# Row maxima from bfloat16 halves, paired float32 score products, and weights joined by exclusive or, in a fused attention and feed-forward kernel

## The chip, the cores and the metric

The kernel runs on one core of a Trainium2 chip. The metric is the time of one execution in device microseconds. Before the change the median of three runs is 602.51 us (601.61 to 602.69). All times here are those of runs and of one profiled execution of the kernel on the chip.

## The reference

Attention over 4 batches, 8 heads, 768 positions and head dimension 64, then a feed-forward layer on its output. Every position sees the first `n_global` = 8 positions and the `n_local` = 96 positions up to itself; each head has a linear bias of its own slope.

```
scores = scale * q @ k.T + bias          # bias = -slope[h] * distance
scores = where(is_global | is_local, scores, -1e9)
a = exp(scores - max); a = a / (sum(a) + 1e-9)
x = (a @ v), heads side by side          # 3072 tokens x 512
h = x @ w_in                             # 512 x 2048, float64
g = h / (1 + exp(-1.702 h))
out = (g @ w_out).astype(float32)        # 2048 x 512, float64
```

The inputs q, k, v are float32. The two weight matrices are float64, so that each of their numbers is two 32-bit words in memory.

## The kernel before, in words

**Planner.** Nearly all the work is a list of tasks. Each task names the engines that may do it with the microseconds that it is thought to take on each, the tasks that it follows, the buffers that it uses, and possibly a due time (`want`) or an earliest time (`soon`). `Work.order` (L104) passes due times back through the list, adds a shift for each group of tasks by its tag (`NUDGE`, L30), and then plays the work through once: at each moment every free engine takes the ready task with the earliest due time whose buffers are free. `LAT` (L47) is the time that it reckons between the end of a task and the start of a task on another engine, and a transfer is reckoned to begin 1.2 us after its issue and to be visible 1.0 us after its end (L171-174). The resulting order is the order of the instructions on each engine. Nothing is reordered when the kernel runs: TensorE takes its matmuls in that order, and all transfers go out from SP's queue in that order, apart from a few. In the first 50 us (`WARM`) the planner gives TensorE filler matmuls (`spare`, L1057; tile `idle`, L1060) whenever it would have nothing to do.

**Attention, first blocks.** The 3072 rows are cut into 24 blocks of 128. Blocks 0 to 3 (`first`, L581) are the first block of each batch, which sees only itself. Their q and k are loaded as float32, turned by TensorE (L422) and scaled into `QZ` and `KF` (L429). Two heads share the 128 partitions, 64 each; `QZ` holds q of one head with zeros in the other's partitions, so that a product with `KF` gives one head. A block then takes these steps. For each head one float32 product (L604) and one bfloat16 product that adds the bias (L605) give the scores; VectorE takes the negated maximum of each row (L609); TensorE turns the maxima (L612). Then the same scores are made once more, transposed, by a float32 product with the operands changed over (L623), the bias (L624) and a product that subtracts the row's maximum (L625). ScalarE's exponential (L636) gives weights that are already turned, and TensorE multiplies them by the values (L631). The result is normalised (`finish`, L653), turned (L689) and split into two float16 halves (L692, L693).

**Attention, other blocks.** Blocks 4 to 23 run in units of two heads (`unit`, L519): scores by float16 halves (L536), row maximum with bias (L542), exponential (L552), split in halves (L556, L557), transfer that turns the tile (L558), values (L567 to L569).

**Weights.** The 16 pieces of 1 MB (`weights`, L357; `w_in` and `w_out` for each of 8 steps) come in through three buffers `ws`. Each float64 is made a float32 from its words: VectorE shifts the high word by 3 (L370, into `wa`); the sign with a fixed exponent goes into the upper half of another tile, on VectorE or ScalarE, whichever the planner picks (L373, L374); ScalarE puts the top bits of the low word in the lower half of it (L375); VectorE adds the two as integers (L376); ScalarE and VectorE then split the sum into float16 halves (L377, L378). The other products of the feed-forward layer use these halves in three products each.

**Feed-forward layer.** The first three chunks of 256 rows are multiplied directly (`up`, L787; `down`, L895). The other nine use a scheme with seven products in place of eight (`up_two`, L827), for which `twist` (L727) forms sums of the weight pieces. The last group of sums overwrites the high-word pieces of four steps (L767, L769).

**Checks.** Squares of q, k, v and of the weights (L404, L998, L1006) and other sums are gathered into one flag, and a general version at the end runs only when the flag says that the inputs are out of the range for which this version holds.

Of the kernel before, what the change touches and what calls it, by code (L numbers as in the profile page):

```python
# [19 lines left out]
P = 128  # L20
# [9 lines left out]
NUDGE = {"T2": -1.5, "down02": 1.4, "down05": -8.2, "down07": -0.8, "down103": 6.7, "down113": -5.5,  # L30
# [9 lines left out]
FIRST = 4  # L40
SIGN = [{"DVE": 0.62, "ACT": 1.0}]
# [5 lines left out]
LAT = 0.3  # L47
MM128, MM256, MM512, MM64, FP128, FP65, TURN = 0.056, 0.109, 0.216, 0.029, 0.216, 0.113, 0.11
# [39 lines left out]
class Work:  # L88
# [15 lines left out]
    def order(self):  # L104
# [25 lines left out]
        while len(done) < len(self.tasks) + spared:  # L130
            moved = False
            for e in free:
# [77 lines left out]
def kernel(  # L210
# [133 lines left out]
    m0 = add({"DVE": 1.3}, distances, [m0], [ints, flt, mk], -4.0)  # L344
    late = add({"POOL": 1.0}, lambda e: None, [m0], want=0.0)
    m0 = add({"DVE": 0.65}, counts, [m0, late])
    covers = add({"DVE": 1.2}, covered, [m0])
    covers.soon = 300.0
    m1 = add({"DVE": 1.1}, own, [m0], [flt, mk])
    M1 = [add({"DVE": 0.6, "ACT": 1.0}, lambda e, f=f: slopes(e, slice(2, 3), range(4 * f, 4 * f + 4)), [m1], [mk]) for f in range(2)]  # L350
    m2 = add({"DVE": 0.7}, other, [m1], [flt, mk])
    M2 = add({"DVE": 2.3, "ACT": 2.6}, lambda e: slopes(e, slice(0, 2)), [m2], [mk])


    WT, W_ready = {}, {}

    def weights(s, u):  # L357
# [7 lines left out]
        part = lambda z: w().bitcast(U16).rearrange("p z (c t) -> p (z c) t", t=2)[:, :, z]  # L365
        t0 = add({"SP": 3.2}, lambda e: load_weights(nc, ws(), w_in, w_out, s, u), bufs=[ws])
# [3 lines left out]
        t2 = add({"DVE": 0.62}, lambda e: nc.vector.tensor_scalar(ai(), ws()[:, :, 1], 3, None, ALU.logical_shift_left),  # L370
                 [t0], [ws, wa])
        t3 = add(SIGN[(2 * s + u) % len(SIGN)], lambda e: (
            nc.vector.tensor_scalar(extra(), ws()[:, :, 1], -2 ** 31, 127 << 23, ALU.bitwise_and, ALU.bitwise_or) if e == "DVE"  # L373
            else nc.scalar.activation(part(1).bitcast(BF16), ws()[:, :, 1].bitcast(F32), AF.Sign)), [t0], [ws, w])  # L374
        t4 = add({"ACT": 1.21}, lambda e: nc.scalar.mul(part(0), ws()[:, :, 0].bitcast(U32), 2.0 ** -29), [t3], [ws, w])  # L375
        t5 = add({"DVE": 1.15}, lambda e: nc.vector.tensor_add(ai(), ai(), extra()), [t2, t3, t4], [w, wa])  # L376
        t6 = add({"ACT": 0.96}, lambda e: nc.scalar.mul(w()[:, 0], wa(), 2.0 * SW), [t5], [wa, w])  # L377
        t7 = add({"DVE": 1.15}, lambda e: nc.vector.scalar_tensor_tensor(  # L378
            w()[:, 1], wa(), 2.0 * SW, w()[:, 0], ALU.mult, ALU.subtract), [t6], [wa, w])
        W_ready[s, u] = t7  # L380

# [7 lines left out]
    blk, prev, checks = {}, {}, []  # L389
# [5 lines left out]
    def load(n, raw, parts=(0, 1, 2)):  # L395
        b, i = place(n)
        return [add({"SP": 1.55}, lambda e, z=z: nc.sync.dma_start(
# [10 lines left out]
    def prep_first(n):  # L408

        raw = Buf(r_raw, [P, 3, H, D], F32, f"raw{n}")  # L410
        QZ = Buf(r_w[NST - 1 - n // 2, n % 2], [P, NU, 2, P], F32, f"QZ{n}")
        KF = Buf(r_hl, [P, NU, P], F32, f"KF{n}", lambda t: t.bitcast(F32).rearrange("p (u t) -> p u t", u=NU))
        d = blk[n] = dict(QZ=QZ, KF=KF, sm=Buf(r_sm, [P, 2 * H], F32, f"sm{n}"))
        zero = add({"POOL": 1.0}, lambda e: [nc.gpsimd.memset(QZ()[D * z:D * z + D, :, 1 - z, :], 0.0) for z in range(2)], bufs=[QZ])
# [166 lines left out]
    def first(n, want):  # L581
# [7 lines left out]
        def products(h):  # L589

            if n < FIRST:
                return [(d["QZ"]()[:, h // 2, h % 2, :], d["KF"]()[:, h // 2, :])]
# [678 lines left out]
```

## Time and profile before

| what | value |
|---|---|
| median of three runs | 602.51 us (601.61 to 602.69) |
| span of the profiled execution, first to last instruction | 600.7 us |
| what lies around the span (runs less span) | 0.9 to 2.0 us |
| granted TensorE clock, mean | 0.997 |
| busy: TensorE, VectorE, ScalarE | 587.5, 503.0, 471.4 us |
| moved by the DMA queues | 109.58 MB, mean 182 GB/s |

The profiled execution's own time is not given beside its span; the runs show how much lies around a span. TensorE is busy for 98% of the span, but its matmuls overlap, and filler counts as busy too. A share of busy time is an average over the whole span; the stages, the timeline and the chain of waits tell more.

### The profile page before, as it was taken

What the parts mean: (1) busy time and instruction counts of PE and PEld (TensorE: products, weight loads), DVE (VectorE), ACT (ScalarE), POOL (GpSimd) and SP (SyncE); (2) the same over time, 40 slices, a digit from 0 to 9 for tenths busy, and PEclk for the clock granted to TensorE, in tenths of its full rate; (3) what the DMA queues carried; (4) which work ended last, traced back from release to release, by engine and by line L of the source; (5) the groups of instructions that cost most, each with busy time, mean ns of one, the idle gap of its engine ahead of it and who ended that gap; (6) DMA issues with size and microseconds to landing.
All of it is one profiled execution on the core that took longest, in us unless ns stands there. A gap on an engine that the chain in (4) does not pass through costs nothing.

```text
span 600.7 us, 17037 instructions
## 1 busy us (share of the span) xinstructions
PE 587.5 (98%) x6816; PEld 445.9 (74%) x6816; DVE 503.0 (84%) x1177; ACT 471.4 (78%) x1098; POOL 5.8 (1%) x18
## 2 busy tenths in 40 slices
PE   8989999999999999999999999999999999999996
PEld 5878767777777867777677777777678768867895
DVE  6998999999999999789699789798979978766532
ACT  3878899978768988888698899788999978944432
POOL 3000000000000000000000000000000000000000
PEclk9999999999999999999999999999999999999998
DMA  8998799999976768979996999999989999920001
GB/s 225 310 251 260 227 253 198 191 179 197 212 141 128 156 117 186 196 145 196 216 206 163 226 209 238 197 233 198 236 186 223 224 193 228 234 40 3 36 1 41
DMA packets 268502, 109.58 MB, mean 182 GB/s; under 512 B 249536, under 2 KB 250048, under 8 KB 268416
## 3 DMA queue, kind: packets, MB, share of 16 engines
q1 hardware_dynamic: 267984, 108.30, 86.6%
q8 instruction: 55, 0.90, 0.7%
q14 instruction: 31, 0.25, 0.1%
q10 hardware_dynamic: 432, 0.13, 0.1%
HBM read 57.67 MB, written 6.29 MB: 106 GB/s over the span
## 4 chain that ended last, share of the span: by engine, by line
PE 85%; DMA 7%; ACT 4%; DVE 2%; issue 1%; SPq 1%; POOL 0%; DVEq 0%; ACTq 0%; POOLq 0%
PE y L895 36%; PE pa L827 14%; PE h L787 10%; PE pb L827 10%; PE s L536 5%; DMA pt<-hl 3%; DMA QK<-QK 2%; PE s L604 1%; PE pv L567 1%; PE pv L569 1%; PE pv L568 1%; PE sT L623 1%; PE idle L1060 1%; DMA xT<-x 1%; DMA out_dram<-yo 1%
## 5 line engine op out<-in xcount | busy, mean ns | idle before, releaser
L895 PE MATMUL y<-w,g 128*128 128x512 f16 (+1 forms) x1248 | 266.8, 363 | 0.0
L895 PEld LDWEIGHTS <-g 128*128 128x128 f16 x1248 | 117.9, 98 | 103.3
L827 PEld LDWEIGHTS <-w 128*128 128x128 f16 x1728 | 101.3, 98 | 5.0
L552 ACT ACTIVATE p<-p,NM 128x232 f32<-128x232 f32 x160 | 76.4, 480 | 7.0 <-DVE NM L542 7.0
L827 PEld LDWEIGHTS <-T 128*128 128x128 f16 x1296 | 77.1, 98 | 6.0
L787 PE MATMUL h<-xT,w 128*128 128x256 f16 x576 | 69.4, 273 | 0.3 <-DMA xT<-x 0.2
L542 DVE CUSTOM_DVE_ANT_0 p<-s,mm 128x232 f32<-128x232 f32 x160 | 57.7, 395 | 8.2 <-PE s L536 7.3
L787 PEld LDWEIGHTS <-w 128*128 128x128 f16 x576 | 55.2, 98 | 9.3 <-issue 0.6
L557 DVE TENSOR_TENSOR hl<-p,hl 128x464 f16<-128x464 f32 x80 | 50.9, 636 | 10.2 <-ACT hl L556 10.1
L868 DVE SCALAR_TENSOR_TENSOR g<-t,g 128x512 f16<-128x512 f32 x72 | 49.3, 687 | 11.1 <-ACT g L867 10.9
L867 ACT ACTIVATE g<-t 128x512 f16<-128x512 f32 x72 | 45.0, 628 | 9.5 <-DVE t L860 8.1
L556 ACT CAST hl<-p 128x464 f16<-128x464 f32 x80 | 46.1, 576 | 6.4 <-DMA pt<-hl 4.4
L859 ACT ACTIVATE t<-h 128x512 f32<-128x512 f32 (+1 forms) x72 | 35.9, 515 | 18.2 <-DVE h L835 15.1
L835 DVE TENSOR_TENSOR h<-pb,h 128x256 f32<-128x256 f32 x72 | 29.6, 420 | 23.0 <-PE pb L827 19.6
L827 PE MATMUL pa<-xS,T 128*128 128x128 f16 x648 | 45.0, 219 | 0.0
L860 DVE SCALAR_TENSOR_TENSOR t<-t,h 128x512 f32<-128x512 f32 (+1 forms) x72 | 38.2, 553 | 4.6 <-ACT t L859 4.0
L536 PEld LDWEIGHTS <-QK 128*128 128x128 f16 x640 | 36.5, 98 | 3.7 <-DMA QK<-QK 0.2
L536 PE MATMUL s<-QK 128*128 128x128 f16 x320 | 38.4, 219 | 0.1
L827 PE MATMUL pb<-xS,w 128*128 128x128 f16 x540 | 37.5, 219 | 0.0
L567 PE MATMUL pv<-VR,pt 128*128 128x64 f16 x288 | 34.8, 193 | 2.6 <-DMA pt<-hl 2.6
L827 PE MATMUL pa<-xT,w 128*128 128x128 f16 x540 | 37.0, 219 | 0.0
L569 PE MATMUL pv<-VR,pt 128*128 128x64 f16 x288 | 34.8, 193 | 0.0
(181 smaller groups left out, 1079.9 us busy)
## 6 DMA issues: line engine op xcount, KB each, us to landing
ws<-in_moe_w_in_dram SPq DMA_DIRECT2D x8, 1024.0 KB
ws<-in_moe_w_out_dram SPq DMA_DIRECT2D x8, 1024.0 KB
raw<-in_q_dram SPq DMA_DIRECT2D x24, 256.0 KB
raw<-in_k_dram SPq DMA_DIRECT2D x24, 256.0 KB
out_dram<-yo SPq DMA_DIRECT2D x22, 256.0 KB
QK<-QK SPq DMA_DIRECT2D x40, 128.0 KB
raw<-in_v_dram SPq DMA_DIRECT2D x20, 256.0 KB
ws_00again<-in_moe_w_in_dram SPq DMA_DIRECT2D x8, 512.0 KB
```

The source lines that it names most:

```text
L536: nc.tensor.matmul(sp()[:, j, lo:hi], d["QK"]()[:, 0, h, :], K[:, 1 + z, h, P - (hi - lo):], start=(z == 0), stop=(z == 1), skip_group_che ...
L542: nc.vector.tensor_tensor_reduce(out=pr()[:, j, :], in0=sp()[:, j, :], in1=m, scale=-1.0 / SC, scalar=3.0e38, op0=ALU.add, op1=ALU.min, ac ...
L552: ex.append(add({"ACT": 0.473}, lambda e, j=j: nc.scalar.activation(pr()[:, j, :], pr()[:, j, :], AF.Exp, bias=NM[:, n, hs[j]:hs[j] + 1], ...
L556: t4 = add({"ACT": 0.5}, lambda e: nc.scalar.copy(hl()[:, 0, :, SKIP:], pr()), ex, [pr, hl])
L557: t5 = add({"DVE": 0.55}, lambda e: nc.vector.tensor_sub(hl()[:, 1, :, SKIP:], pr(), hl()[:, 0, :, SKIP:]), [t4], [pr, hl])
L567: nc.tensor.matmul(o, ph, V[:, 0, h], start=(s == 0), stop=False, skip_group_check=True)
L569: nc.tensor.matmul(o, pl, V[:, 0, h], start=False, stop=(s == ns - 1), skip_group_check=True)
L787: nc.tensor.matmul(ph()[:, fi, :], w1(s, cc, z, fi), X[:, y, cc, :], start=(j + cc == 0), stop=(j == 2 and cc == NCC - 1))
L827: nc.tensor.matmul(o()[:, fi], w, x()[:, y * NCC + 2 * k + cc, t], start=(first and fi + j + cc == 0), stop=(last and j + cc == 3), skip_g ...
L867: t4 = add({"ACT": 0.53}, lambda e, g=g, tt=tt: nc.scalar.mul(g()[:, 0], tt(), SG / (SX * SW)), u, [tt, g])
L868: t5 = add({"DVE": 0.61}, lambda e, g=g, tt=tt: nc.vector.scalar_tensor_tensor(g()[:, 1], tt(), SG / (SX * SW), g()[:, 0], ALU.mult, ALU.s ...
L895: nc.tensor.matmul(y(), part(zg, f), w2(s, z, f % 2)[:, m], start=(begin and f + j == 0), stop=(end and j == 2 and f == 2 * len(steps) - 1 ...
```

## The change

1. **Row maxima from bfloat16.** In blocks 0 to 3 the scores from which the maxima are taken use the upper 16 bits of each float32 word of q and k, read in place as bfloat16 with a step of two. The transposed scores stay float32.
2. **Two heads in one product.** `QZ` is laid out with the two heads of a pair outermost, and the transposed scores of both heads come from one float32 product of 256 columns with `KF` as the stationary operand.
3. **Weights joined by exclusive or.** The sign step is always VectorE's; the separate shift is gone; one instruction shifts the high word and joins it to the rest by exclusive or. The low bits are scaled by 0.9365, so that they can't round up into the next bit. The exponent is then right without a factor of two.
4. **Checks.** The squares of the weights are taken with the weights themselves, four of them early, and the last sums of `twist` wait for them. Bounds of the checks are tighter.
5. **Masks.** The masks of the other blocks (L340) become four tasks of two heads each, wanted by 34 us, in place of one task of eight.
6. **Planner.** Durations of many tasks, `LAT` (0.3 to 0.2), the timing of transfers, and all the shifts of `NUDGE` are new.

```diff
-NUDGE = {"T2": -1.5, "down02": 1.4, "down05": -8.2, "down07": -0.8, "down103": 6.7, "down113": -5.5,
...
+NUDGE = {"T3": 12.3, "block0": -11.9, "block13": -0.8, "block2": -18.8, "block4": 7.7, "block7": -8.8,
...
-SIGN = [{"DVE": 0.62, "ACT": 1.0}]
+LAST = 0.9365
...
-LAT = 0.3
-MM128, MM256, MM512, MM64, FP128, FP65, TURN = 0.056, 0.109, 0.216, 0.029, 0.216, 0.113, 0.11
+LAT = 0.2
+MM128, MM256, MM512, MM64, FP128, FP65, TURN = 0.056, 0.109, 0.216, 0.029, 0.264, 0.21, 0.11
...
-                    dma = max(dma, now + 1.2) + us
-                    t.end = dma + 1.0
+                    dma = max(dma, now + 1.95) + us
+                    t.end = dma + 0.9
...
-    M2 = add({"DVE": 2.3, "ACT": 2.6}, lambda e: slopes(e, slice(0, 2)), [m2], [mk])
+    M2 = [add({"DVE": 0.41, "ACT": 0.6}, lambda e, f=f: slopes(e, slice(0, 2), range(2 * f, 2 * f + 2)), [m2], [mk], 34.0) for f in range(4)]
...
-        t2 = add({"DVE": 0.62}, lambda e: nc.vector.tensor_scalar(ai(), ws()[:, :, 1], 3, None, ALU.logical_shift_left),
-                 [t0], [ws, wa])
-        t3 = add(SIGN[(2 * s + u) % len(SIGN)], lambda e: (
-            nc.vector.tensor_scalar(extra(), ws()[:, :, 1], -2 ** 31, 127 << 23, ALU.bitwise_and, ALU.bitwise_or) if e == "DVE"
-            else nc.scalar.activation(part(1).bitcast(BF16), ws()[:, :, 1].bitcast(F32), AF.Sign)), [t0], [ws, w])
-        t4 = add({"ACT": 1.21}, lambda e: nc.scalar.mul(part(0), ws()[:, :, 0].bitcast(U32), 2.0 ** -29), [t3], [ws, w])
-        t5 = add({"DVE": 1.15}, lambda e: nc.vector.tensor_add(ai(), ai(), extra()), [t2, t3, t4], [w, wa])
+        t3 = add({"DVE": 0.61}, lambda e: nc.vector.tensor_scalar(
+            extra(), ws()[:, :, 1], -2 ** 31, -2 ** 30, ALU.bitwise_and, ALU.bitwise_xor), [t0], [ws, w])
+        t4 = add({"ACT": 1.21}, lambda e: nc.scalar.mul(low(), ws()[:, :, 0].bitcast(U32), LAST * 2.0 ** -29), [t3], [ws, w])
+        t5 = add({"DVE": 1.15}, lambda e: nc.vector.scalar_tensor_tensor(
+            ai(), ws()[:, :, 1], 3, extra(), ALU.logical_shift_left, ALU.bitwise_xor), [t3, t4], [ws, w, wa])
...
+        early_ = s % 2 and u == 0
+        checks.append(add({"ACT": 1.05}, lambda e: nc.scalar.activation(
+            junk, w()[:, 0], AF.Square, accum_out=swt[:, u, s:s + 1]), [t7], [w], 140.0 if early_ else 270.0 + 18.0 * (2 * s + u)))
+        squared[s, u] = checks[-1]
...
-        QZ = Buf(r_w[NST - 1 - n // 2, n % 2], [P, NU, 2, P], F32, f"QZ{n}")
+        QZ = Buf(r_w[NST - 1 - n // 2, n % 2], [P, 2, NU, P], F32, f"QZ{n}")
...
+        def upper(a):
+            return a.bitcast(BF16).rearrange("p (t z) -> p t z", z=2)[:, :, 1]
...
+                        if n < FIRST:
+                            qp, kp = upper(qp), upper(kp)
                         nc.tensor.matmul(sp()[:, j], qp, kp, start=(z == 0), stop=False, skip_group_check=True)
...
-                    for z, (qp, kp) in enumerate(products(h)):
-                        nc.tensor.matmul(o, kp, qp, start=(z == 0), stop=False, skip_group_check=True)
+                    if n < FIRST:
+                        if j % 2 == 0:
+                            nc.tensor.matmul(sT()[:, j:j + 2, :], d["KF"]()[:, h // 2, :], d["QZ"]()[:, :, h // 2, :],
+                                             start=True, stop=False, skip_group_check=True)
...
-                             [t3, *used], [f, w])
+                             [t3, *used, squared[o, 0]], [f, w])
```

More of the change, by code (lines that the diff above doesn't have):

```diff
@@ L382, in w1 @@
+        squared[s, u] = checks[-1]
+        if not early_:
+            checks[-1].soon = 200.0 + 18.0 * (2 * s + u)
     def w1(s, cc, z, fi):
@@ L432, in prep_first @@
         rows = [slice(D * z, D * z + D) for z in range(2)]
-        d["qk_ready"] = [zero, *(taken(lambda z=z: QZ()[rows[z], :, z, :], 0, rows[z]) for z in range(2)), taken(KF, 1, slice(0, P))]
+        d["qk_ready"] = [zero, *(taken(lambda z=z: QZ()[rows[z], z], 0, rows[z]) for z in range(2)), taken(KF, 1, slice(0, P))]
     def own_values(n):
```

66 lines of the change are left out of this document (33 added, 33 removed), and 13 rows, old and new, of the table NUDGE.

## The prediction

> **What bounds the kernel now.** I read the page first, then busy time by stage, then the timeline of the early stage.
>
> ```profile
> span 600.7 us, 17037 instructions
> ...
> PE 587.5 (98%) x6816; PEld 445.9 (74%) x6816; DVE 503.0 (84%) x1177; ACT 471.4 (78%) x1098; POOL 5.8 (1%) x18
> ...
> PE 85%; DMA 7%; ACT 4%; DVE 2%; issue 1%; SPq 1%; POOL 0%; DVEq 0%; ACTq 0%; POOLq 0%
> ```
>
> TensorE is busy 98% of the span and is 85% of the chain that ended last. Busy is not the same as useful, so next come the busy times by stage (columns: stage, its length, busy time of each engine with its instructions, granted clock, DMA share, GB/s) and the filler matmuls:
>
> ```profile
> 0.00:40.00 40.00, 35.02 (x269) 28.24 (x270) 32.88 (x76) 24.54 (x35) 5.77 (x18) 1.00 0.93 262
> 40.00:120.00 80.00, 80.00 (x703) 61.06 (x701) 75.23 (x136) 73.53 (x126) 0.00 (x0) 1.00 0.98 228
> 120.00:250.00 130.00, 129.79 (x1492) 95.52 (x1491) 122.98 (x283) 106.58 (x256) 0.00 (x0) 1.00 0.91 168
> 250.00:500.00 250.00, 247.35 (x3191) 184.61 (x3190) 214.08 (x545) 215.38 (x562) 0.00 (x0) 1.00 1.02 204
> 500.00:580.00 80.00, 80.00 (x991) 62.63 (x990) 52.69 (x128) 46.15 (x111) 0.00 (x0) 1.00 0.44 90
> 580.00:601.00 21.00, 15.37 (x182) 13.81 (x179) 5.10 (x16) 5.25 (x12) 0.00 (x0) 0.92 0.10 30
> ```
>
> ```profile
> L1060 PE MATMUL idle<-idle 128*128 128x512 bf16 x26 | 9.2, 476 | 2.9 <-ACT hl L429 1.6 <-POOL idle L252 1.3
> ```
>
> Before 40 us TensorE is idle 40 - 35.02 = 5.0 us and spends 9.2 us on filler. From 40 to 580 it is idle 0.21 + 2.65 = 2.9 us in 540. After the last matmul some 5 us remain. So from 40 us on, each microsecond of TensorE work that disappears is a microsecond of time, as long as the other engines can feed it earlier. They are not idle: in 40 to 120 us VectorE is busy 75.23 of 80 and ScalarE 73.53 of 80. TensorE's own work in the blocks 0 to 3 is what the change cuts, and it lies in 10 to 52 us, half in the stage with filler and half in the dense one.
>
> **The score products.** Rows of the timeline, with starts first, one head after another, then twelve float16 matmuls of 128 columns in the chain of waits:
>
> ```profile
> 13.01 0.44 PE L604 MATMUL s<-hl,QZ 128*128 128x128 f32 x2
> 13.28 0.22 PE L605 MATMUL s<-mm,id 128*128 128x128 bf16 x1
> 13.34 0.44 PE L604 MATMUL s<-hl,QZ 128*128 128x128 f32 x2
> ```
>
> ```profile
> 563.46 0.67 PE pa L827 x12
> ```
>
> A float32 product of 128 columns is two instructions. It holds TensorE 0.277 us (13.01 to 13.28) and the bias product 0.056 (13.28 to 13.34), together 0.333 us a head. A packed 16-bit product takes 0.67/12 = 0.056. The change reads the upper halves of the float32 words as bfloat16, one instruction, so a head falls to 0.112 us. There are 8 heads in 4 blocks: 32 x 0.221 = 7.1 us less. No row of the trace has a 16-bit operand that skips every other element. Its bounds are the packed 0.056 and one float32 instruction's 0.109 (below), which also takes one 4-byte word a column: 32 x 0.053 = 1.7 us less gain. I take 0.056, because the kind of instruction is that of the packed row.
>
> The Trainium skill bears on this in two places. "Advanced Engine Details and Errata", section SBUF Cachelines, says that reads lose nothing while at least two fall in one 16-byte line; a step of 4 bytes gives four, so by it the sum stays 7.1. "TensorE: Matmul & The Clock Gate", section Back-to-back issue gap, gives some 81 ns for a 128-column matmul in a stream of load and matmul pairs; by it the gain would be 32 x (0.333 - 0.162) = 5.5 us, but this trace has 56 ns in such a stream, so it stays a doubt about the strided case alone.
>
> **The turned products.** Here two heads share one stationary operand and stream 256 columns:
>
> ```profile
> 16.54 0.44 PE L623 MATMUL sT<-QZ,hl 128*128 128x128 f32 x2
> 16.82 0.22 PE L624 MATMUL sT<-id,mm 128*128 128x128 bf16 x1
> 16.87 0.22 PE L625 MATMUL sT<-mT,id 128*128 128x128 bf16 x1
> 16.93 0.44 PE L623 MATMUL sT<-QZ,hl 128*128 128x128 f32 x2
> ...
> 28.94 1.04 PE L422 MATMUL tq<-ident,raw 128*128 128x128 f32 x8
> ```
>
> ```profile
> L623 PEld LDWEIGHTS sT<-QZ,hl 128*128 128x128 f32 x64 | 9.8, 191 | 0.3
> ```
>
> A head takes 0.39 us now (16.54 to 16.93), two heads 0.777. Eight float32 instructions back to back take 1.04 us with the last one's drain of about 0.17, so one streams in 0.109; of the pair's 0.277 some 0.06 is weight loading that the stream didn't cover. With 256 columns the two instructions stream 2 x 0.218 = 0.436, and a load of 0.191 now fits behind a stream of 0.218. Two heads become 0.436 + 4 x 0.056 = 0.66 with the load covered, 0.72 with one exposed, 0.78 with two: a gain of 0.12, 0.06 or 0 for each of 16 pairs, so 0 to 1.9 us. I take the middle of the first two, 0.09 x 16 = 1.4. Together TensorE's work falls by 7.1 + 1.4 = 8.5 us.
>
> **The weights.** Groups by shape (busy, mean ns, idle before):
>
> ```profile
> L376 DVE CUSTOM_DVE_ANT_0 wa<-wa,w 128x2048 uint16<-128x2048 uint16 x16 | 19.5, 1223 | 2.3 <-ACT w L375 1.9
> L378 DVE SCALAR_TENSOR_TENSOR w<-wa,w 128x1024 f16<-128x1024 f32 x16 | 19.3, 1217 | 0.1
> ...
> L374 ACT ACTIVATE w<-ws 128x1024 bf16<-128x1024 f32 x9 | 12.2, 1355 | 0.0
> ...
> L370 DVE TENSOR_SCALAR wa<-ws 128x1024 int32<-128x1024 int32 x16 | 11.0, 685 | 0.0
> ...
> L373 DVE TENSOR_SCALAR w<-ws 128x1024 int32<-128x1024 int32 x7 | 4.8, 688 | 0.0
> ```
>
> The shift (L370) goes into the joining instruction: 11.0 us off VectorE. The sign step, 9 times on ScalarE (12.2 us) and 7 times on VectorE, is now VectorE's 16 times: 9 x 0.688 = 6.2 us on. The joining instruction becomes a two-tensor one with two operations; the nearest row, L378, has 1.217 us against the 1.223 of the integer addition: no difference. So VectorE falls by 4.8 us and ScalarE by 12.2, all before 120 us. By itself this is worth nothing at the end, as both hide under TensorE there, but it is the cover that lets TensorE's gain count: 4.8 us less in a stage where VectorE had 80 - 75.23 = 4.8 us free. Without it the earlier demand would eat that slack.
>
> One thing gets worse. The joining instruction now reads the loaded words, so a load buffer (three of them) is free only after it, not after the ScalarE step before it:
>
> ```profile
> 20.23 1.36 ACT L375 ACTIVATE w<-ws 128x1024 uint16<-128x1024 uint32 x1
> ```
>
> ```profile
> 21.62 1.41 SPq L206 DMA_DIRECT2D ws<-in_moe_w_in_dram  x1
> ```
>
> The fifth load was issued at 21.62, just as that step ended at 21.59. It would now go out 1.2 us later or more, and behind it on SP's queue the loads of q and k. Bounds: nothing where the plan holds the load back anyway, up to 13 loads over 3 buffers x 1.22 = 5.3 us for the last weight. I take nothing: the step of 0.69 that vanishes ahead of it (L370) or the 1.36 (L374) gives it back.
>
> **The first chain.** It decides whether the half of the gain that lies before 31 us is kept. The chain of waits from 22 to 31 us, and the masks of the other blocks:
>
> ```profile
> 22.34 0.60 ACT pt L636
> 22.94 1.25 ACT w L374
> 24.18 1.20 ACT w L375
> ...
> 29.47 0.42 ACT xT L692
> ...
> 32.76 1.31 PE h L787 x12
> ```
>
> ```profile
> 11.19 1.69 DVE L340 TENSOR_SCALAR mm<-mk 128x256 bf16<-128x256 f32 x8
> ```
>
> Up to 22 us the chain is TensorE's score products of blocks 0 and 1, then ScalarE's weight steps. Half of the 8.5 us (4.25) goes from the first part, and ScalarE's sign step of 1.25 from the second. The eight mask instructions (1.69 us) stood on VectorE ahead of the first maxima; they become four tasks wanted by 34 us on either engine, so they needn't stand there. All three links of this chain get shorter, so I count the whole half, with 0 as its lower end.
>
> **The checks.** Four weight squares must now come before the last twisted matrix overwrites those weights:
>
> ```profile
> L998 ACT ACTIVATE junk<-w 128x1024 bf16<-128x1024 f16 x16 | 16.8, 1048 | 0.1
> ```
>
> 4 x 1.05 us on ScalarE, before 250 us instead of spread later; in 120 to 250 us it has 130 - 106.58 = 23 us free. If that cover were gone, 4.2 us. The final sums keep their number of instructions, the zeroing on POOL is as large as before: nothing.
>
> **The dates.** The new durations and dates reorder every queue. Their bounds are from removing the 2.9 us idle of 40 to 580 us and a few us of the first stage's 14.2 to adding as much; I take 0.
>
> Sum: 602.5 - 7.1 - 1.4 = **594.0 us**. The profiled span is 600.7, and the runs lie 0.9 to 2.0 above it, so the profile after should show a span near 592.2.
>
> **Rivals.** *The front half is lost* (0.14): the first stage waits for loads and VectorE (32.88 of 40 busy, DMA share 0.93) and more filler takes the place of blocks 0 and 1; only 4.25 remains, 598.3. For it: filler of 9.2 us shows that this stage had time to spare; against it: the chain above. *Strided reads cost like float32* (0.10): 594.0 + 1.7 = 595.7. *The dates win more* (0.17): idle of 2.9 goes and 1.5 us of filler, 589.6; for it, the planner's costs now lie nearer the rows (LAT aside), against it, the 540 us were dense already. *Nothing arrives* (0.04): VectorE or the DMA (share 0.98 in 40 to 120 us) sets the pace and TensorE gets idle for what it sheds, 602.5.
>
> *Slower* (0.06): TensorE takes its queue in order, and the values products wait for a transposed tile:
>
> ```profile
> PE pv L567 <- DMA pt<-hl: 2.6, 3, 1.1
> ```
>
> ```profile
> pt<-hl SPq DMA_TRANSPOSE x80
> ```
>
> There are 80 such handovers, and three of them cost 2.6 us now. The plan reckons 0.1 us less (0.3 to 0.2) at each handover between engines, of which a unit has five, so a unit may be placed up to 0.5 us too early. A mean delay over 8.5/80 = 0.11 us a unit eats the gain; at 0.2 the time is 602.5 - 8.5 + 16 = 610.0. Against it: the plan's transfers get longer by 0.65 us (1.2 to 1.95, 1.0 to 0.9), which places the products later, and the waits now are rare.
>
> **How the numbers follow.** The forecast has 0.49, with its own range 592 to 596 from the bounds of the turned products and small changes of idle. The range runs from 589.5 to 598.8: it takes in the strided reads, most of the lost front half and the better half of the dates' case, and leaves out the last two cases and the far ends of those, some 2 in 10. A change under 0.2% (1.2 us) can't be told from none here. Faster holds all but the last two cases: 0.90; same 0.04; slower 0.06.
>
> **What would show it.** The score line of blocks 0 to 3 with one bfloat16 instruction a head, starts 0.11 us apart for a head and its bias (0.16 if strided reads cost). The turned products in 32 instructions of 256 columns, a pair of heads 0.66 to 0.72 us apart. Filler and idle before 40 us together still near 14 us; over 18 would mean that the front half is lost. Idle from 40 us on near 3 us; over 11 would mean the slower rival. VectorE near 498 us, ScalarE near 459. Weight loads issued no later, one by one, than now. The forecast is wrong if the first products of the dense layer, at 32.8 us now, don't start some 4 us sooner while filler grows.

## The result and the profile after

The changed kernel takes 598.37 us, the median of four runs (597.32 to 599.74). The kernel before takes 602.6 us beside it (four runs, 601.61 to 604.23). The ratio is 0.9926, 95% interval 0.9902 to 0.9949. That is 4.2 us less, where 8.5 were forecast: the time lies at the upper end of the range, 589.5 to 598.8, and outside the forecast's own range of 592 to 596.

The page of the kernel after: its span, the busy times, and the shares of the chain that ended last.

```profile
span 597.2 us, 16877 instructions
...
PE 578.5 (97%) x6741; PEld 435.2 (73%) x6742; DVE 496.0 (83%) x1167; ACT 463.6 (78%) x1092; POOL 5.8 (1%) x18
...
PE 73%; DMA 14%; DVE 6%; ACT 3%; issue 2%; SPq 1%; ACTq 0%; DVEq 0%
```

TensorE is busy 9.0 us less (587.5 to 578.5), more than forecast, since there is less filler too. The span of the profiled executions fell by only 3.5 us (600.7 to 597.2). The chain has changed: TensorE's part fell from 85 to 73%, that of transfers doubled from 7 to 14%. Busy time by stage of the kernel after (columns as in the prediction) tells where:

```profile
0.00:40.00 40.00, 34.70 (x297) 27.65 (x299) 32.10 (x74) 29.29 (x47) 5.76 (x18) 1.00 0.99 270
40.00:120.00 80.00, 78.94 (x684) 56.30 (x682) 74.92 (x140) 67.01 (x123) 0.00 (x0) 1.00 1.07 244
120.00:250.00 130.00, 130.00 (x1581) 98.82 (x1580) 125.36 (x294) 111.25 (x275) 0.00 (x0) 1.00 0.90 159
250.00:500.00 250.00, 243.32 (x3073) 178.90 (x3071) 208.20 (x524) 208.57 (x537) 0.00 (x0) 1.00 1.08 205
500.00:580.00 80.00, 80.00 (x1004) 63.41 (x1002) 50.93 (x125) 43.53 (x104) 0.00 (x0) 1.00 0.37 82
580.00:601.00 21.00, 11.56 (x114) 10.09 (x111) 4.45 (x16) 4.00 (x9) 0.00 (x0) 0.89 0.09 30
```

From 40 to 580 us TensorE now idles 1.06 + 6.68 = 7.7 us; before it was 2.9. Nearly all of it lies in 250 to 500 us, far behind the blocks that the change made shorter. Busy time hides part of such gaps, because a matmul counts as busy while it drains. For a ledger I therefore counted from the starts of all matmuls in the trace: the time from one start to the next is work (or filler) up to what that form of matmul takes back to back, and waiting beyond that. What is taken for back to back is a choice: with the median spacing of each form, useful work falls by 8.3 us and the waiting of 250 to 500 us goes from 3.7 to 8.6, so a row is good to about 1 us. Each column is one profiled execution; what is missing to the span is 1.3 us ahead of the first matmul and 5.6 to 5.9 us behind the last.

| us | before | after | difference |
|---|---|---|---|
| TensorE's useful work | 575.3 | 567.9 | -7.4 |
| filler | 8.9 | 5.7 | -3.2 |
| waiting before 40 us | 4.3 | 4.7 | +0.4 |
| waiting 40 to 250 us | 0.7 | 2.2 | +1.5 |
| waiting 250 to 500 us | 4.2 | 9.1 | +4.9 |
| waiting behind 500 us | 0.3 | 0.4 | +0.1 |

The sum is -3.7; the spans differ by -3.5. So the work went nearly as forecast, the first stage did better, and some 6.5 us of new waiting behind 40 us took more than half of it back.

Single instructions of the kernel after, in the timeline of TensorE (start, time, instruction):

```profile
10.86 0.22 PE L618 MATMUL s<-hl,QZ 128*128 128x128 bf16 x1
10.92 0.22 PE L619 MATMUL s<-mm,id 128*128 128x128 bf16 x1
10.97 0.22 PE L618 MATMUL s<-hl,QZ 128*128 128x128 bf16 x1
...
13.62 0.65 PE L638 MATMUL sT<-QZ,hl 128*128 128x256 f32 x2
14.10 0.22 PE L643 MATMUL sT<-id,mm 128*128 128x128 bf16 x1
...
14.33 0.65 PE L638 MATMUL sT<-QZ,hl 128*128 128x256 f32 x2
...
28.01 2.78 PE L806 MATMUL h<-xT,w 128*128 128x256 f16 x24
```

A score product and its bias start 0.11 us apart (10.86 to 10.97), a turned pair takes 0.71 (13.62 to 14.33), and the first products of the dense layer start at 28.01. Before, they start at 32.60 in the timeline of TensorE (the prediction's row of the chain, 32.76, begins a few matmuls later). The groups by shape of the kernel after:

```profile
L378 DVE SCALAR_TENSOR_TENSOR wa<-ws,w 128x1024 int32<-128x1024 int32 x16 | 19.3, 1217 | 1.4 <-ACT w L377 1.4
...
L375 DVE TENSOR_SCALAR w<-ws 128x1024 int32<-128x1024 int32 x16 | 10.8, 683 | 1.5 <-DMA ws<-in_moe_w_in_dram 1.3 <-DMA ws<-in_moe_w_out_dram 0.2
...
L638 PE MATMUL sT<-QZ,hl 128*128 128x256 f32 x32 | 10.3, 403 | 0.0
...
L1075 PE MATMUL idle<-idle 128*128 128x512 bf16 x15 | 5.2, 487 | 1.4 <-POOL idle L257 1.3
```

Filler fell from 26 to 15 instructions (9.2 to 5.2 us busy). The shift and exclusive or take 1.217 us, as the row that was used for them. What TensorE waited for, in the kernel after (total, times, longest):

```profile
PE pv L576 <- DMA pt<-hl: 2.9, 4, 1.3
PE pv L576 <- DMA VR<-VG: 2.3, 1, 2.3
...
PE pb L846 <- DVE h L854: 0.9, 2, 0.5
PE s L545 <- DVE NM L551: 0.8, 2, 0.5
```

The first two stop the values products: one on the turned tile, the other on the global rows of the values. All of the first three and 0.5 us of the fourth lie in 250 to 500 us, together 6.6 of the 6.68 us idle there. Before, the turned tile alone stood in that stage, with 2.6 us. So the named wait for the turned tile grew by only 0.3 us; the new idle time is the one wait for the global rows (2.3) and those for VectorE (1.4). The longest one can be followed. First the order of issues on SP's queue of the kernel after, then TensorE, then the chain of waits:

```profile
367.64 0.57 SPq L211 DMA_DIRECT2D ws_00again<-in_moe_w_in_dram  x1
368.30 1.23 SPq L567 DMA_TRANSPOSE pt<-hl  x1
369.59 0.73 SPq L406 DMA_DIRECT2D over<-in_v_dram  x1
370.41 1.42 SPq L668 DMA_DIRECT2D VR<-VG  x1
371.92 0.47 SPq L932 DMA_DIRECT2D out_dram<-yo  x1
372.45 0.47 SPq L406 DMA_DIRECT2D raw<-in_v_dram  x1
373.01 3.77 SPq L567 DMA_TRANSPOSE pt<-hl  x1
```

```profile
373.56 0.83 PE L846 MATMUL pb<-xT,w 128*128 128x128 f16 x12
376.72 0.19 PE L576 MATMUL pv<-VR,pt 128*128 128x64 f16 x1 [2.33 <-DMA VR<-VG]
```

```profile
360.70 6.16 DMA pt<-hl
...
370.41 6.18 DMA VR<-VG
```

The transfer of 16 KB, `VR<-VG`, took 6.18 us from the start of its issue to its landing, 1.42 of them for the issue, behind half a megabyte of `ws_00again` and 256 KB of `over`. TensorE stood 2.33 us for it. `ws..again` is the second reading of the weights: from 265 us on all 16 pieces are read again in 32 transfers of 512 KB, for the check of their squares and smallest values alone. Nothing that TensorE does needs it.

### The profile page after: what moved, and what is told of

Same layout as the page of the kernel before. It is cut to its first block, busy times and chain, and to the rows that moved or that the text cites. A ratio compares the mean times of both kernels' runs of the same rounds, so it can differ in the third digit from the quotient of the medians.

```text
span 597.2 us, 16877 instructions
## 1 busy us (share of the span) xinstructions
PE 578.5 (97%) x6741; PEld 435.2 (73%) x6742; DVE 496.0 (83%) x1167; ACT 463.6 (78%) x1092; POOL 5.8 (1%) x18
## 4 chain that ended last, share of the span: by engine, by line
PE 73%; DMA 14%; DVE 6%; ACT 3%; issue 2%; SPq 1%; ACTq 0%; DVEq 0%
PE y L914 31%; PE pa L846 12%; PE pb L846 9%; PE h L806 8%; DMA pt<-hl 6%; PE s L545 4%; DMA QKover<-QKover 2%; PE pv L576 1%; PE sT L638 1%; PE pv L578 1%; PE pv L577 1%; DMA QKover<-qk16over 1%; DMA VR<-VG 1%; DMA again<-in_k_dram 1%; DVE hl L566 1%
## 5 line engine op out<-in xcount | busy, mean ns | idle before, releaser
L914 PE MATMUL y<-w,g 128*128 128x512 f16 (+1 forms) x1248 | 264.6, 363 | 0.8 <-DVE w L381 0.5
L914 PEld LDWEIGHTS <-g 128*128 128x128 f16 x1248 | 118.2, 98 | 107.3 <-DVE g L818 1.4
L561 ACT ACTIVATE p<-p,NM 128x232 f32<-128x232 f32 x160 | 76.6, 481 | 10.5 <-DVE NM L551 10.2
L806 PE MATMUL h<-xT,w 128*128 128x256 f16 x576 | 67.1, 273 | 0.0
L806 PEld LDWEIGHTS <-w 128*128 128x128 f16 x576 | 55.6, 98 | 8.1
L576 PE MATMUL pv<-VR,pt 128*128 128x64 f16 x288 | 34.6, 193 | 3.6 <-DMA VR<-VG 2.3
L576 PEld LDWEIGHTS <-pt 128*128 128x128 f16 x320 | 29.5, 98 | 10.2 <-DMA pt<-hl 4.0
```

Source lines behind the costliest of these rows:

```text
L561: ex.append(add({"ACT": 0.473}, lambda e, j=j: nc.scalar.activation(pr()[:, j, :], pr()[:, j, :], AF.Exp, bias=NM[:, n, hs[j]:hs[j] + 1], ...
L576: nc.tensor.matmul(o, ph, V[:, 0, h], start=(s == 0), stop=False, skip_group_check=True)
L806: nc.tensor.matmul(ph()[:, fi, :], w1(s, cc, z, fi), X[:, y, cc, :], start=(j + cc == 0), stop=(j == 2 and cc == NCC - 1))
L914: nc.tensor.matmul(y(), part(zg, f), w2(s, z, f % 2)[:, m], start=(begin and f + j == 0), stop=(end and j == 2 and f == 2 * len(steps) - 1 ...
```

## The experiments

Three theories were stated. *Theory 1*: the work shed arrives, and the missing time is stalls that belong to the new order of the instructions. *Theory 2*: it doesn't arrive, since the other engines can't feed TensorE sooner, whatever the order. *Theory 3*, within the first: the stalls come from the second reading of the weights, which shares SP's queue and the transfer engines with the turned tiles. All ratios are against the kernel before on the same chip.

### Float32 products in the new order

```diff
-                        if n < FIRST:
-                            qp, kp = upper(qp), upper(kp)
...
-                    if n < FIRST:
-                        if j % 2 == 0:
-                            nc.tensor.matmul(sT()[:, j:j + 2, :], d["KF"]()[:, h // 2, :], d["QZ"]()[:, :, h // 2, :],
-                                             start=True, stop=False, skip_group_check=True)
-                    else:
...
+                    for z, (qp, kp) in enumerate(products(h)):
+                        nc.tensor.matmul(o, kp, qp, start=(z == 0), stop=False, skip_group_check=True)
```

> The changed kernel with the order of every queue kept, but blocks 0 to 3 compute both score products per head in float32 again (8.1 us more work for TensorE by the rows of the two traces). Theory 1 (the stalls of TensorE after 40 us, 11.7 us against 5.2 before, belong to the new order): they stay near 11.7 us and the time rises by about 8, to 606. Theory 2 (the other engines and transfers can't feed TensorE any earlier, whatever the order): the stalls shrink by about as much as TensorE comes later, to 5 us or less, and the time stays within 2 us of 598.4.

Measured: 601.83 us, ratio 1.0015 (1.0001 to 1.0029). The products are thus worth 1.0015 - 0.9926 = 0.009, some 5.3 us, in the new order; TensorE's useful work is 575.8 us, 7.9 more than after. The time lies between the two that were expected (606 and about 598.4): most of the products' gain arrives, not all of it. The waiting of 250 to 500 us is 2.6 us, against 9.1 in the kernel after. That stage of this kernel:

```profile
250.00:500.00 250.00, 249.09 (x3173) 184.27 (x3171) 213.45 (x543) 213.80 (x558) 0.00 (x0) 1.00 1.05 208
```

TensorE idles 0.9 us here in place of 6.7, with the same order and the same transfers. So the stalls don't belong to the order alone: work that comes earlier runs into something that did not come earlier with it. SP's queue shows where. Both kernels issue the same 361 transfers in the same order. The kernel after is 7.7 us ahead at its 268.8 us (`QK<-QK`, 276.43 here), 5.9 ahead at 364, 3.2 at 410 and 1.0 at 495: the lead melts in this stage. How much of it melts varies from run to run. The profiled execution here is the fastest of its ten (600.13). In this pair of executions only 1.2 us of the 7.9 are left in the span (598.4 against 597.2), while by all runs 5.3 us arrive. And the rest of the change (weights, masks, order), without the products, brought nothing.

### The new products in the old order

```diff
+        def upper(a):
+            return a.bitcast(BF16).rearrange("p (t z) -> p t z", z=2)[:, :, 1]
...
+                        if n < FIRST:
+                            qp, kp = upper(qp), upper(kp)
...
+                            nc.tensor.matmul(sT()[:, j:j + 2, :], d["KF"]()[:, h // 2, :], d["QZ"]()[:, h // 2, :, :],
+                                             start=True, stop=False, skip_group_check=True)
...
```

> The kernel before with its order of every queue, in which blocks 0 to 3 alone get the new products (bfloat16 for the maxima, two heads in one float32 product); weights, masks, dates as before. Theory 1: the gain arrives, 594.5 us if the first stage passes on all 8.1 us, 598.5 if its half before 31 us turns into waiting for the weights' steps on ScalarE; the stalls after 40 us stay near 5 us. Theory 2: stalls after 40 us rise by 4 us or more, and the time is 598.5 or more though the first stage has gained.

Measured: 601.27 us, ratio 1.0001 (0.9981 to 1.002): nothing, though the useful work is 566.9 us, 8.4 less than before. Its first stage, and in it the chain of waits and TensorE (the line numbers are those of this kernel):

```profile
0.00:40.00 40.00, 32.23 (x239) 23.39 (x240) 34.13 (x78) 26.03 (x37) 5.76 (x18) 0.97 0.97 270
```

```profile
20.81 1.23 DVE wa L376
...
23.20 0.60 DVE wa L370
...
23.94 1.22 DVE wa L376
25.17 0.60 DVE w L373
...
34.10 1.22 DVE wa L376
35.32 0.60 DVE top L614
```

```profile
35.98 0.27 PE L617 MATMUL aux<-ident,top 128*8 128x128 f32 x1 [2.25 <-DVE top L614]
...
37.42 2.21 PE L797 MATMUL h<-xT,w 128*128 128x256 f16 x12
```

Here the front half is lost: waiting before 40 us doubled from 4.3 to 8.6 us. The chain runs through VectorE's weight steps, the shift (L370), the sign (L373) and the addition (L376), which stand in its queue ahead of the maxima (L614) that TensorE waits for. Part of the count is not waiting but a slower clock. From 37.98 us on, 2 us after the wait of 2.25, the trace grants TensorE half its clock for 3.41 us, which costs 1.7 us:

```profile
36.00:40.00 4.00, 3.49 (x23) 2.63 (x24) 3.97 (x6) 3.50 (x6) 0.00 (x0) 0.75 1.12 244
40.00:44.00 4.00, 4.00 (x38) 3.54 (x37) 3.86 (x6) 3.35 (x4) 0.00 (x0) 0.83 0.90 254
```

The mean granted clock of the ten runs is 0.996, where that of the kernel before beside them is 0.998, so the profiled execution is no exception. Neither expectation came true as it was stated: the gain did not arrive, but it was lost in the first stage, and the waiting behind 40 us rose by only 2 us. That the other engines can't feed TensorE sooner (theory 2) holds for the old order in the first stage. In the kernel after, where VectorE has fewer of these steps and another order, the waiting there is 4.7 us, and the profiled execution keeps its clock.

### A light second reading in the new kernel

```diff
...
+    nc.sync.dma_start(ws[:, 0:64].rearrange("p f t -> p (f t)"), words[half * n:half * n + P, 0:128])
...
-                t0 = add({"SP": 1.6}, lambda e, s=s, u=u, ws=ws, half=half: load_weights(nc, ws(), w_in, w_out, s, u, half), bufs=[ws])
+                t0 = add({"SP": 1.6}, lambda e, s=s, u=u, ws=ws, half=half: load_eighth(nc, ws(), w_in, w_out, s, u, half), bufs=[ws])
...
```

> The changed kernel with the order kept; the second reading of the weights for the checks (from 265 us on, 16.8 MB) fetches an eighth of the bytes, and the sums and minima of that check are made from this eighth, repeated, at nearly the old cost. Left out: seven eighths of this check. Theory 3 (turned tiles come late because the transfers of the second reading stand ahead of them): the stalls of 250 to 500 us, 9.1 us now, fall to 4 or less and the time to 593 to 594. Theories 1 and 2: stalls as before within 1.5 us, time 597 to 599.

Measured: 590.7 us in three runs, ratio 0.9821 (0.9789 to 0.9854). A fourth run took 3444.5 us, which suggests that the flag sent it through the general version; why was not settled, and it is left out. The number, kind and order of the instructions are those of the kernel after; each second reading moves 64 KB in place of 512. The stage by busy time, and the wait of the kernel after that was followed above:

```profile
250.00:500.00 250.00, 249.89 (x3158) 183.90 (x3157) 214.34 (x544) 212.26 (x553) 0.00 (x0) 1.00 0.86 162
```

```profile
PE pv L583 <- DMA VR<-VG: 0.3, 1, 0.3
```

TensorE's idle time there goes from 6.68 to 0.11 us, the counted waiting from 9.1 to 1.2, and neither the turned tile `pt` nor VectorE's `h` stands among the waits any longer. The transfers go out in the same order as in the kernel after, within 2.5 us of it up to 372 us, and some 8 us sooner from 487 on. The bytes of the second reading cost the kernel after 0.9926 - 0.9821 = 0.0105, about 6.3 us (some 2.4 either way, from the two intervals).

### The shift as an instruction of its own

```diff
-        t5 = add({"DVE": 1.15}, lambda e: nc.vector.scalar_tensor_tensor(
-            ai(), ws()[:, :, 1], 3, extra(), ALU.logical_shift_left, ALU.bitwise_xor), [t3, t4], [ws, w, wa])
+        t5 = add({"DVE": 1.15}, lambda e: [
+            nc.vector.tensor_scalar(ai(), ws()[:, :, 1], 3, None, ALU.logical_shift_left),
+            nc.vector.scalar_tensor_tensor(ai(), ai(), 0, extra(), ALU.logical_shift_left, ALU.bitwise_xor)],
+            [t3, t4], [ws, w, wa])
```

> The changed kernel with the order kept, but the shift is an instruction of its own on VectorE again (0.685 us more for each of 16 pieces of weights, 11.0 us in all before 115 us). If VectorE's relief is the cover that lets TensorE's gain count: the time rises by 3 to 8 us, to 601 to 606, with new stalls of TensorE between 20 and 120 us. If VectorE had room there anyway: within 1.5 us of 598.4.

Measured: 602.68 us, ratio 1.002 (1.0002 to 1.0039), 0.0094 or 5.7 us more than the kernel after, for 16 x 0.685 = 11 us more of VectorE. The stage in which it stands:

```profile
40.00:120.00 80.00, 76.03 (x644) 53.58 (x642) 78.42 (x142) 64.70 (x114) 0.00 (x0) 1.00 1.00 230
```

VectorE is busy 78.42 of 80 us, and TensorE idles 3.97 us against 1.06. From 30 to 125 us the chain of waits runs mostly through VectorE (its weight steps L383, L380 and L379 alone are 39% of it), where in the kernel after it runs mostly through TensorE (L806 and L914, 49%). So VectorE has no room for the shift, as the prediction had it. The edit adds 11 us, though, while the change frees 4.8 on VectorE by the prediction's count and 7.0 by the two profiles (503.0 to 496.0); what those are worth was not measured. And 1.7 us of this execution, at 384 us, are again a stretch of 3.41 us at half clock, behind a wait of 2.29 us; in four of the ten runs the mean clock is 0.999, and these have 601.04 to 603.31 us.

### The light second reading in the kernel before

The edit is that of the light second reading above, in the kernel before.

> The kernel before, order kept, with the second reading of the weights cut to an eighth of its bytes, as was done to the changed kernel (which fell to 590.9 us, ratio 0.9821 to the kernel before). Left out: seven eighths of that check. If the transfers of the second reading cost both kernels alike: about 595 us (ratio 0.990), stalls of 250 to 500 us from 4.2 to 1 us or so, and the change would be worth 4.5 us with or without them. If the changed kernel pays more for them (theory 3: it gives back its gain there): 598 us or more (ratio 0.995 or above), and with light rereads the change is worth 7 us or more, near the 8.1 that TensorE sheds.

Measured: 599.1 us, ratio 0.9968 (0.9957 to 0.9979). The kernel before pays 1.9 us (some 0.7 either way) for the same bytes, less than the kernel after beyond the noise, as was expected if the change gives back its gain there:

```profile
250.00:500.00 250.00, 250.00 (x3236) 187.40 (x3235) 216.12 (x553) 217.30 (x568) 0.00 (x0) 1.00 0.84 158
```

TensorE has no idle time left in this stage. Without those bytes the change is worth 0.9821/0.9968 = 0.9853 (0.982 to 0.989, from the two intervals), or 8.8 us, next to the 8.5 forecast.

### The light second reading with the old order and the new products

This joins the edits of the second experiment and of the light second reading, in the kernel before.

> The old order with the new products, and with the second reading cut to an eighth of its bytes (left out: seven eighths of that check). The old order with full reading gained nothing: 4.7 us of the 8.1 went into more waiting before 40 us, the rest into stalls later. If those later stalls came from the reading: 595 to 596 us (599.1 less the 3.4 that pass the first stage). If the old order gives them back anyway: 598 to 599.

Measured: 597.3 us, ratio 0.9936 (0.9916 to 0.9956). Against the kernel before with a light second reading (0.9968) the products are now worth 0.3%, 1.9 us of 8.4. That is between the two times that were expected. The waiting before 40 us is 8.5 us and the filler 9.5, and the stretch at half clock is here too (3.41 us from 36.09 on). In the old order the first stage loses most of the gain, whatever the second reading does.

### The second reading later

All three edits leave nothing out; they move the earliest times that the plan gives to the second reading. The planner then lays the whole order anew, so these kernels differ from the kernel after in the order of other instructions too; the light reading kept that order. First, all of it later and a little denser:

```diff
-                    e2[:, 1, o:o + 1], hi_w(), axis=AX.X, op=ALU.min), [t1], [ws], 275.0 + 8.0 * o))
-                t0.soon = 265.0 + 8.0 * o
+                    e2[:, 1, o:o + 1], hi_w(), axis=AX.X, op=ALU.min), [t1], [ws], 340.0 + 7.2 * o))
+                t0.soon = 330.0 + 7.2 * o
```

> The changed kernel with the second reading of the weights planned from 330 to 553 us instead of 265 to 513, one every 7.2 us, with everything that it reads and checks. The planner lays the whole order anew. Theory 3: the stalls move later and shrink, since after 500 us the DMA share is 0.37; time 594 to 597. Theory 1 (the stalls belong to the order, wherever the transfers are): 597 to 600.

Measured: 595.13 us, ratio 0.9892 (0.9866 to 0.9918). Then at half the pace up to 457 us, and faster behind it, so that 15 of the 32 transfers go out behind 500 us in place of 4:

```diff
+                at = 265.0 + 16.0 * (2 * (2 * s + u) + half)
+                at = min(at, 457.0 + 5.0 * (2 * (2 * s + u) + half - 12))
...
-                t0.soon = 265.0 + 8.0 * o
+                t0.soon = at
```

> The changed kernel with the second reading thinned where the attention's tiles are turned (one every 16 us from 265 to 441) and the other twenty pieces from 457 to 552 us, one every 5 us, nothing left out. Theory 3: stalls of 250 to 460 us fall by half or more, to 3 us; time 592 to 596, if VectorE and ScalarE carry the checks after 500 us without a stall. Theory 1: 597 to 600.

Measured: 591.86 us, ratio 0.9837 (0.9811 to 0.9863); the four runs lie between 590.5 and 595.93, and the profiled one is the slowest. Last, slower still (8 of the 32 ahead of 457 us in place of 23), and the checks' second loads of q, k and v moved behind 500 us:

```diff
-            t.soon = 400.0 + 30 * n
+            t.soon = 500.0 + 14 * n
...
+                at = 265.0 + 24.0 * (2 * (2 * s + u) + half)
+                at = min(at, 457.0 + 4.0 * (2 * (2 * s + u) + half - 8))
...
```

> The changed kernel with the second reading moved further: one piece every 24 us from 265 to 433 us, the others every 4 us from 457 to 549, and the second reading of q, k and v of blocks 0 to 3 from 500 us on instead of 400. Theory 3: stalls of 250 to 500 us from 3.0 (two paces) to about 1.5 and the time 590 to 592; if VectorE or ScalarE can't carry the checks after 500 us, new stalls there and 593 or more.

Measured: 592.0 us, ratio 0.9839 (0.9798 to 0.9879). Two stages of this last kernel:

```profile
250.00:500.00 250.00, 249.04 (x3181) 184.58 (x3179) 205.50 (x523) 201.57 (x510) 0.00 (x0) 1.00 0.88 173
500.00:580.00 80.00, 80.00 (x968) 63.97 (x966) 57.95 (x135) 54.66 (x138) 0.00 (x0) 1.00 0.73 183
```

The share of the transfer engines falls from 1.08 to 0.88 in the dense stage and rises from 0.37 to 0.73 in the one after it, where TensorE hardly waits. TensorE's idle time from 250 to 500 us falls from 6.68 to 0.96. These two versions beat both kernels; between them there is no difference to be measured.

### The two paces in the kernel before

The edit is that of the two paces, in the kernel before.

> The kernel before with the second reading at two paces (one piece every 16 us from 265 to 441 us, the other twenty from 457 to 552), nothing left out, the order laid anew by the old plan. With an eighth of the bytes it had gained 1.9 us, so if the reading is all that this touches: 599 to 601 us (ratio 0.997 to 1.000), and the 591.9 us of the changed kernel with the same pace is the change's gain coming through. If the pace is worth 6 us by itself: 595 us.

Measured: 602.14 us, ratio 1.0013 (0.9993 to 1.0034): no gain, where 599 to 601 us were expected. In the kernel before, with an order laid anew by its own plan, these dates are worth nothing; in the changed kernel they are worth 5.3 us (0.9926 - 0.9837). That fits a TensorE which the products have made early, but the two plans differ in durations and shifts too.

### The old durations of transfers in the plan

```diff
-                    dma = max(dma, now + 1.95) + us
-                    t.end = dma + 0.9
+                    dma = max(dma, now + 1.2) + us
+                    t.end = dma + 1.0
...
-        t0 = add({"SP": 2.75}, lambda e: load_weights(nc, ws(), w_in, w_out, s, u), bufs=[ws])
+        t0 = add({"SP": 3.2}, lambda e: load_weights(nc, ws(), w_in, w_out, s, u), bufs=[ws])
...
```

> The changed kernel with the transfers' old reckoning in the plan (1.2 and 1.0 us of latency, 3.2 us for a piece of weights, 1.55 for a block of q, k or v), all else as changed; the order is laid anew. If the new, shorter transfer costs crowd the queue and make the turned tiles late: stalls of 250 to 500 us fall from 9.1 to 5 us, time 594 to 597. If not: 598 us or more, since the dates were fitted to the new costs.

Measured: 606.03 us, ratio 1.0082 (1.0059 to 1.0105), worse than both. Filler is 10.25 us, the waiting 40 to 250 us 8.8 and 250 to 500 us 6.5. So undoing the plan's new durations of transfers does not bring the gain back. But the shifts per tag were left as they are in the changed kernel, and a plan with other durations gives them other effects, so this run doesn't price the durations by themselves. It also has 3.41 us at half clock, from 27.96 us on.

### The count of waiting in all kernels

By the ledger's count (us; one execution each, where runs of one kernel lie up to 5.4 us apart; time lost at half clock counts mostly as waiting):

| kernel | useful | filler | before 40 | 40 to 250 | 250 to 500 | behind 500 |
|---|---|---|---|---|---|---|
| float32 products, new order | 575.8 | 6.0 | 3.8 | 2.2 | 2.6 | 1.1 |
| new products, old order | 566.9 | 9.35 | 8.6 | 2.65 | 4.0 | 0.7 |
| after, light reading | 567.2 | 6.4 | 4.7 | 2.3 | 1.2 | 0.5 |
| after, shift apart | 567.2 | 5.95 | 6.0 | 7.4 | 8.1 | 0.6 |
| before, light reading | 575.3 | 9.0 | 4.3 | 0.5 | 0.5 | 0.3 |
| old order, new products, light | 567.1 | 9.5 | 8.5 | 2.1 | 0.75 | 0.4 |
| after, reading later | 568.0 | 5.8 | 4.6 | 2.1 | 5.1 | 1.7 |
| after, two paces | 567.9 | 5.9 | 4.4 | 3.9 | 3.0 | 1.3 |
| after, later still | 567.9 | 5.9 | 4.4 | 1.7 | 2.4 | 0.3 |
| before, two paces | 575.3 | 9.0 | 4.3 | 1.8 | 1.6 | 1.9 |
| old durations of transfers | 567.8 | 10.25 | 3.4 | 8.8 | 6.5 | 0.6 |

## Why the prediction was right or wrong

**Score products: right.** 0.11 us a head was forecast with its bias, and 10.86 to 10.97 shows it. The rival that strided reads cost like float32 falls: it would have shown 0.16.

**Turned products: mis-sized by a little.** The term was the middle of one load exposed and none, 0.09 x 16 = 1.4 us. A pair takes 14.33 - 13.62 = 0.71 us, which is the case of one load exposed: (0.777 - 0.71) x 16 = 1.1 us. With the scores some 8.1 us, against 8.5; the ledger has 7.4 in this execution and 7.9 to 8.4 in the three pairs of kernels that differ by the products alone.

**Weights: right but for one sign.** The shift and exclusive or takes 1.217 us as forecast, VectorE is busy 496.0 us (498 forecast), ScalarE 463.6 (459 forecast; 1.6 us of masks went there, which is a part of it). That VectorE has no time to spare there was argued in the prediction and is shown by the separate shift, +5.7 us. "Weight loads issued no later, one by one, than now" did not come true: by their place in the row 12 of the 16 go out later, the third at 17.98 in place of 9.33 us, the fifteenth at 91.89 in place of 79.54. The fifth, of which the prediction speaks, is 0.3 us later, and the last 5 us sooner. Whether the longer hold of the load buffers or the new order makes them late, and what it costs, was not tried by itself.

**The first chain: right, and better than counted.** The front half was counted whole. The first products of the dense layer start some 4.6 us sooner (28.01 against 32.60), filler fell by 3.2 us in the ledger where none was counted on, and waiting before 40 us rose by 0.4 only. The rival "the front half is lost" had 598.3 us as its time, next to the 598.37 measured, but its mechanism is not what happened: filler and idle before 40 us are 5.2 + 5.3 = 10.5, not over 18. Number and mechanism must be told apart. That the time still lies inside the range is luck in part: the upper end, 598.8, was drawn around this rival and not around the term that failed, and the 3.2 us less filler, on which the prediction had not counted, offset half of the new waiting. The mechanism does exist: in the old order with the new products the front is where the gain is lost.

**The dates: the step that failed.** "The dates, I take 0", with bounds of which the upper one was "to adding as much", is the term that took the missing time. Idle from 40 to 580 us was to stay near 3; it is 7.7, and the counted waiting behind 40 us went from 5.2 to 11.7 us. The place is 250 to 500 us, and the waits hang on the second reading of the weights: with its bytes cut to an eighth the waiting there is 1.2 us, the time 590.7. The slower rival was near in kind, with values products that wait for a transfer, but not the same: the named wait for the turned tile is 2.9 us where it was 2.6, and one wait for the global rows (2.3 us) and some for VectorE (1.4) make the rest of the idle time. Nor was its cause the one named there. The rival blamed the plan's handovers between engines; the light reading keeps that plan and its order, and 0.11 us of idle time is left. Its counterargument was incomplete too: the plan's transfers got 0.65 us more latency, but a piece of weights is reckoned at 2.75 us in place of 3.2 and a block of q, k or v at 1.35 in place of 1.55, so that in a row of transfers each takes less.

The row that could have warned of it was quoted: a DMA share of 1.02 in 250 to 500 us. Only the shares of the first two stages (0.93 and 0.98) were used. TensorE shedding 8 us early asks for the later tiles 8 us sooner, out of a stage whose transfers were already at 1.02. The float32 products in the new order fit this: they come to the stage 7.7 us later and leave it 1.0 us later, with 2.6 in place of 9.1 us of waiting. The share is a warning and no measure of the waits, since that kernel has 1.05 and idles 0.9 us.

**What stays open.** Why the same bytes cost the kernel after 6.3 us and the kernel before 1.9 is only argued. Being early explains part. But the new products in the old order wait just 4.0 us in that stage, and there the lead is already lost: on SP's queue 2.4 us of the 8.4 are left at 96 us, and none at 251, ahead of the second reading. Whether the order of the issues on SP's queue or the rate of the transfer engines ends these waits was not told apart: the light reading relieves both. In the one wait followed above, 4.8 of the 6.2 us passed behind the end of the issue.

## What to carry to other kernels

Work taken off the bounding engine arrives only as far as everything behind it can come earlier as well: look for the stage, however far behind the edit, whose transfers are full, and ask what there could be done later. Work that nothing waits for, such as a check's second reading, belongs where the transfer engines are idle (here behind 500 us); in the changed kernel that was worth 5.3 us, as much as the change itself, and in the kernel before nothing. A time that agrees with a rival is no proof of it; its place in the trace is.

## What the hardware showed that was not expected

A bfloat16 operand that takes every other element costs nothing here, not even where both operands do so: score and bias products start 0.05 to 0.06 us apart (10.86, 10.92, 10.97), like packed ones. This agrees with the Trainium skill, "Advanced Engine Details and Errata", section SBUF Cachelines; the 81 ns a matmul of "TensorE: Matmul & The Clock Gate", section Back-to-back issue gap, is not seen.

Soon after a wait TensorE's clock was halved in four of the profiled executions, each time for 3.41 us, which is 1.7 us of work: from 37.98 us in the old order with the new products (wait 2.25 us), from 36.09 with the light reading beside it (2.25), from 384.06 with the separate shift (2.29) and from 27.96 with the old durations of transfers (1.61). The wait of 2.33 us in the kernel after was not followed by it. What decides was not tried.

A transfer that turns a tile can hold SP's queue three times as long as usual. The groups of that line in the kernel after give its issue time (shortest, median, longest in ns):

```profile
L567 SPq DMA_TRANSPOSE pt<-hl x80: 1231/1262/3772, 78.2 to 520.8; - x80
```

The longest, 3.77 us, is the one that was issued at 373.01, behind four other transfers in 3.4 us; whatever follows on the queue is issued that much later. With the light second reading the same place in the queue took 1.67 us, but 4.47 us is the longest in that kernel, at 97.5 us, so the second reading is not all that stretches it.
